# A later landing estimate for w2's size passes, attention work ahead of forced steps, and w2's sums ahead of the next group's

## The chip, the cores and the metric

The kernel runs on one core of one Trainium2 chip. The metric is the device time of one execution in microseconds; the kernel before took 1533.35 us (median of three runs). The engines are TensorE (PE, with its weight load PEld), VectorE (DVE), ScalarE (ACT), GpSimd (POOL) and SyncE (SP, which here issues nearly all loads). The TensorE clock was granted in full (1.00) throughout.

## The reference

Two layers act on x of 2048 tokens and 1024 features. Each adds first an attention branch (A) and then a gated feed-forward branch (B), both on a layer-normalised input. All weights are shared by the two layers.

```python
def A(x, wqkv, wo):                       # 32 heads of 32
    q, k, v = split(x @ wqkv)             # 1024 -> 3 x 1024
    # token s sees tokens s, s-2, ..., s-14 (8 of them, masked below 0)
    attn = softmax(sum_d(q[s] * k[s - off]) * 32 ** -0.5)
    return sum_w(attn * v[s - off]) @ wo  # 1024 -> 1024
def B(x, w1, w3, w2):                     # 1024 -> 3584 -> 1024
    return (silu(x @ w1) * (x @ w3)) @ w2

x = x + A(layernorm(x)); x = x + B(layernorm(x))    # layer 0
x = x + A(layernorm(x)); x = x + B(layernorm(x))    # layer 1
```

## The kernel before

**Stages.** The tokens are cut into four chunks of 512. First comes layer 0's query, key and value projection for all chunks (`q_part`, products L836, copies out of PSUM L840), 0 to 192 us. Then follow eight units u = 0 to 7, one for each layer and chunk, which do branch B (`b_stage`). Attention for the next unit runs meanwhile on DVE (`score_steps`: products L590, maximum L625, difference L628, exponential on ACT L629, sum L634, reciprocal L636, quotient L637; `value_steps`: L665; folds L510, L512, L514), with the projection wo on PE as `o_tile` (L771, added to x in L776). From u = 1 on, layer 1's projections for one chunk come between two units.

**Two forms of branch B.** Units 0 and 1 (to 514 us) multiply with w1 (L1279), w3 (L1288) and w2 (L1310) as they are. During them the other engines prepare weights for units 2 to 7. These use a scheme of seven products on 2 x 2 blocks in place of eight (P1 to P7, run by `pipeline` L1052 and, for w2, by `W` L1165), which needs sums and differences of weight blocks, kept in DRAM. In the seven-product form ACT copies or applies silu to product sums between the products (L1064, L1069, L1073, L1227, L1232; for w2 L1173, L1181, L1185), DVE adds (L1076, L1088, L1236; L1188), and PE's next product waits for these where it reuses a PSUM bank. P7, for instance, adds to the bank that L1073 (or L1185 for w2) has copied out after P6.

**Preparing the weights.** For a group of w1 or w3, `weight_size` squares the tile on ACT (L878) to size a scale; PE sums over partitions into a side bank, DVE reduces it (L884). `weight_sums` scales four blocks on ACT (L910), `differences` forms three more on DVE (L923), and POOL stores them. For w2 the size comes from the whole matrix: `part_of_w2` loads eight pieces of w2 in layer 0's projection stage into the idle tile hT (L973), and `measure2` squares each piece in two passes on ACT (L958). After the sixteenth pass `total_scale` (L993) makes the scale. Only then can `sums_of_w2` (L1009 on ACT, L1015 on DVE) form w2's blocks, from w2 tiles that unit 0 or 1 has loaded (L722).

**Order.** PE, DVE, ACT and SP execute in the order in which the program emits instructions, which Python settles when the kernel is built. `now` is a clock of estimates with one time for each of `pe`, `dve`, `act`, `sp` and `dma`; the functions of those names advance it. Work that isn't in the main chain stands in queues of generators, which yield an estimated cost, a time when ready, and the step. `background(until)` takes the DVE queues' steps (`makes`, `norms`, `adds`, `values`, `scores`) that fit before a time. `act_background()` takes ACT steps from `acts`, `sizes` (L958), `parts` (L878) and `reads` (L910, L1009), each while its estimated end lies no more than 2.2 us past PE's clock:

```python
if s is None or max(now["act"], s[1]) + s[0] > now["pe"] + gate[0]:
    break
```

`head(queue)` gives a queue's first step, or nothing when that generator is blocked. `release_held` frees w1 and w3 tiles once their group's sums are all emitted; `held` lists the (matrix, group) pairs that wait for that, `made` those that are done, and `finish_sums(done)` forces steps from `reads`, `parts` and `makes` until it is so. PSUM has six banks for the main products and two side banks, for `po` (L771), for the attention logits and for the sizes. Loads into SBUF go through SP's one queue: weights (L707 wqkv, L712, L718, L722), the transposes of normalised tokens (xn from L269 on DVE, or L318 and L345 on ACT; L272 transposes on a DMA), and attention's reads.

Of the kernel before, what the change touches and what calls it, by code (L numbers as in the profile page):

```python
# [17 lines left out]
def kernel(  # L18
# [95 lines left out]
    def head(queue):  # L114

        while queue:
            item = queue[0]
            if item[1] is None:
                item[1] = next(item[0], StopIteration)
                if item[1] is StopIteration:  # L120
                    queue.pop(0)
                    continue
            if item[1] == "blocked":
                item[1] = None
                return None
            return item[1]
        return None
# [173 lines left out]
    adds, acts, makes, reads, parts, sizes = [], [], [], [], [], []  # L301
# [53 lines left out]
    def take_act(queue):  # L355
        cost, ready, emit = queue[0][1]
        act(cost, ready)
        queue[0][1] = None
        emit()
# [338 lines left out]
    def load_weight(pieces=1):  # L698

        if len(w_tiles) == len(seq):  # L700
            return
        kind, i, n, *rest = seq[len(w_tiles)]
        if kind == "qkv":
            w = wp.tile([P, KH, D], BF16, name="wqkv", tag="w")
            step = KH // pieces
            for k0 in range(0, KH, step):
                nc.sync.dma_start(w[:, k0:k0 + step, :],  # L707
                                  wqkv_v[:, n * KH + k0:n * KH + k0 + step, i * D:(i + 1) * D])
            at = dma(1024, now["pe"]) if len(w_tiles) > 5 else 33.0
        elif kind == "t2":  # L710
            w = wp.tile([P, 8, 512], FP16, name="t2", tag="w")
            nc.sync.dma_start(w[:, 0:rest[0], :], t2_d[i][:, n])  # L712
            at = dma(128 * rest[0], now["pe"])
        elif kind in ("early", "late"):
            early = kind == "early"
            w = wp.tile([P, 2, 4 if early else 3, KT // 2, P], FP16, name=kind, tag="w")
            v = t_d[i][n][:, 0:8] if early else t_d[i][n][:, 8:14]
            nc.sync.dma_start(w[:], v.rearrange("p (a b) k c -> p a b k c", a=2))  # L718
            at = dma(1024 if early else 768, now["pe"])
        elif kind == "w2":  # L720
            w = wp.tile([P, 8, 512], BF16, name="w2t", tag="w")
            nc.sync.dma_start(w[:, 0:n, :], w2_v[:, i:i + n, rest[0] * 512:(rest[0] + 1) * 512])  # L722
            at = dma(128 * n, now["pe"])
        else:
            w = wp.tile([P, KT, FG * P], BF16, name=kind + "t", tag="w")
            v = w1_v if kind == "w1" else w3_v
            nc.sync.dma_start(w[:, :, 0:n * P], v[:, :, i * P:(i + n) * P])
            at = dma(1200, now["pe"])
            if rest[0]:
                got = {}  # L730
                parts.append([weight_size(*rest[0], w, at, got), None])
                reads.append([weight_sums(*rest[0], w, got), None])
        w_at[len(w_tiles)] = at
        w_tiles.append(w)

# [194 lines left out]
    def finish_sums(done):  # L930

        while not done():
            if head(reads) is not None:
                take_act(reads)
            elif head(parts) is not None:
                take_act(parts)
            elif head(makes) is not None:
                take(makes)
            else:
                pe_requests(1, True)  # L940

# [23 lines left out]
    def part_of_w2():  # L965

        i = len(w2_parts) - len(unread)
        while len(measured) < 2 * i:
            assert head(sizes) is not None
            take_act(sizes)  # L970
        if unread:
            g0, n, hh = unread.pop(0)
            nc.sync.dma_start(hT[:, 0:n, :], w2_v[:, g0:g0 + n, hh * 512:(hh + 1) * 512])  # L973
            sizes.append([measure2(i, n, dma(128 * n, now["pe"])), None])

    unread = list(w2_parts)

# [275 lines left out]
    def b_stage(u, hold):  # L1253

        l, c = units[u]
        last = l == 1
        ready = ready_norm(("B", l, c))
        xnT = xnTs[("B", l, c)]
        for (f0, f1) in fsplits:
            lastsplit = (f1 == fsplits[-1][1])  # L1260
            if u >= TU:
                products(u, f0, f1, hold)
                continue
            for g0 in range(f0, f1, FG):
                gn = min(FG, f1 - g0)
                w1t, w3t = weight("w1"), weight("w3")
                release_held(1)
                for fi in range(gn):
                    f = g0 + fi
                    slack = 1.0 if f < f1 - 2 else -0.5  # L1270
                    if f < f1 - 1:
                        between(hold)
                    else:
                        flush()
                    if f == 8 and 1 <= u and u + 3 < len(units):
                        queue_q(u + 3)
                    pg = bank("pg")
                    for kk in range(KT):
                        nc.tensor.matmul(pg[:], lhsT=w1t[:, kk, fi * P:(fi + 1) * P], rhs=xnT[:, kk, :],  # L1279
                                         start=(kk == 0), stop=(kk == KT - 1))  # L1280
                    r = pe(KT, ready)
                    sg = sgp.tile([P, CH], BF16, name="sg")
                    nc.scalar.activation(sg[:], pg[:], ACTF.Silu)
                    ts = act(0.5, r, "silu")
                    act_background()
                    pu = bank("pu")
                    for kk in range(KT):
                        nc.tensor.matmul(pu[:], lhsT=w3t[:, kk, fi * P:(fi + 1) * P], rhs=xnT[:, kk, :],  # L1288
                                         start=(kk == 0), stop=(kk == KT - 1))
                    r = max(pe(KT), ts)  # L1290
                    background(r + slack)
                    nc.vector.tensor_tensor(hT[:, f - f0, :], sg[:], pu[:], op=ALU.mult)
                    th = dve(0.64, r)
                    release_held(2)
                held.append((u, g0 // FG))
                release_held(1)
            if lastsplit:
                xnT_free["B", l, c] = now["pe"]
            split, nq = fsplits.index((f0, f1)), (f1 - f0) // 2
            flush()  # L1300
            got = [(weight("w2", False), w_at[used[0] - 1]) for _ in range(4)]
            release_held(1)
            tiles, times = [[[got[2 * hh + fh][i] for fh in range(2)] for hh in range(2)] for i in range(2)]
            for hh in range(2):
                now["pe"] = max(now["pe"], *times[hh])
                for j in range(TPC):
                    n, step = c * TPC + j, TPC * hh + j
                    acc = psum.tile([P, 512], FP32, name="acc", tag="mm")
                    for f in range(f1 - f0):
                        nc.tensor.matmul(acc[:], lhsT=hT[:, f, j * P:(j + 1) * P],  # L1310
                                         rhs=tiles[hh][f // nq][:, f % nq, :],
                                         start=(f == 0), stop=(f == f1 - f0 - 1))
                    pe(f1 - f0 - 1)
                    r = pe(1, th)
                    if step == 2:
                        release_held(0)
                    if step == 0:
                        steps = range(u * nq // 2, (u + 1) * nq // 2)
                        reads.extend([sums_of_w2(split, f, tiles, max(times[0] + times[1])), None] for f in steps)
                    act_background()  # L1320
                    background(r + 1.0)
                    dve(0.64, r)
                    xs = x_sb[:, n, hh * 512:(hh + 1) * 512]
                    nc.vector.tensor_tensor(xs, xs, acc[:], op=ALU.add)
                    if j == TPC - 1 and hh == 1:
                        finish_sums(lambda: all(("w2", split, f) in made for f in steps))
                        release(4)
                    between(hold and not lastsplit, lastsplit and hh == 0 and j == 1 and not hold)
        if u == TU - 1:
            force(makes, lambda: not any(pending))  # L1330
            scale_h()
            sums_free[:] = [0.0] * 3
# [80 lines left out]
```

## Time and profile before

| | us |
|---|---|
| median of three runs | 1533.35 |
| lowest, highest | 1532.43, 1533.71 |
| the profiled execution, its own time | 1532.7 |
| its span in the trace | 1531.0 |
| PE busy | 1518.1 (99%) |
| DVE busy | 1201.8 (78%) |
| ACT busy | 884.1 (58%) |
| POOL busy | 153.7 (10%) |

The span runs from the first to the last instruction in the trace; 1.7 us of the execution lie around it. A row of the timeline has the start and the duration in us, the engine, the line, the operation, and output and inputs by their names in the program; brackets give the idle time ahead of it and what ended it. A row of the waits has the waiting engine and line, what it waited for, total us, times and the longest. A row of the stretches has the length, the busy time of PE, PEld, DVE, ACT and POOL with counts, the granted clock, the DMA share and GB/s.

### The profile page before, as it was taken

What the parts mean: (1) busy time and instruction counts of PE and PEld (TensorE: products, weight loads), DVE (VectorE), ACT (ScalarE), POOL (GpSimd) and SP (SyncE); (2) the same over time, 40 slices, a digit from 0 to 9 for tenths busy, and PEclk for the clock granted to TensorE, in tenths of its full rate; (3) what the DMA queues carried; (4) which work ended last, traced back from release to release, by engine and by line L of the source; (5) the groups of instructions that cost most, each with busy time, mean ns of one, the idle gap of its engine ahead of it and who ended that gap; (6) DMA issues with size and microseconds to landing.
All of it is one profiled execution on the core that took longest, in us unless ns stands there. A gap on an engine that the chain in (4) does not pass through costs nothing.

```text
span 1531.0 us, 25095 instructions
## 1 busy us (share of the span) xinstructions
PE 1518.1 (99%) x9594; PEld 989.5 (65%) x9634; DVE 1201.8 (78%) x2126; ACT 884.1 (58%) x1388; POOL 153.7 (10%) x308
## 2 busy tenths in 40 slices
PE   9999999999999999999999999999999999999999
PEld 7666644444444577575786767766677767686865
DVE  4688998889989898989698958898678986435445
ACT  3885476567665357455565564756557445554643
POOL 1210102121211101001011010100111000000000
PEclk9999999999999999999999999999999999999999
DMA  9777969798997888979779997898969988878885
GB/s 321 202 218 215 253 226 330 272 304 289 306 320 247 280 316 294 347 264 303 263 269 324 346 268 282 280 323 302 323 225 333 338 296 282 306 272 334 318 294 203
DMA packets 261432, 439.56 MB, mean 287 GB/s; under 512 B 73856, under 2 KB 201088, under 8 KB 245056
## 3 DMA queue, kind: packets, MB, share of 16 engines
q1 hardware_dynamic: 248464, 390.90, 76.8%
q0 software_dynamic: 12704, 46.93, 8.6%
q8 instruction: 75, 1.23, 0.3%
q14 instruction: 45, 0.37, 0.1%
q10 hardware_dynamic: 144, 0.13, 0.0%
HBM read 345.90 MB, written 67.90 MB: 270 GB/s over the span
## 4 chain that ended last, share of the span: by engine, by line
PE 97%; ACT 1%; issue 1%; DVE 0%; DMA 0%; SPq 0%; ACTq 0%
PE st L1052 32%; PE ps L836 21%; PE w L1165 16%; PE po L771 7%; PE pg L1279 6%; PE pu L1288 6%; PE acc L1310 6%; PE pq L444 1%; PE L L604 0%; DMA wqkv<-in_A_wqkv_dram 0%; ACT L629 0%; ACT L1227 0%; ACT E L629 0%; ACT sg L1227 0%; DVE x_sb L1150 0%
## 5 line engine op out<-in xcount | busy, mean ns | idle before, releaser
L836 PE MATMUL ps<-xnT,wqkv 128*128 128x512 f16 (+1 forms) x1469 | 320.4, 379 | 0.2
L1052 PEld LDWEIGHTS <-early 128*128 128x128 f16 x2688 | 262.6, 98 | 40.4 <-issue 3.5
L836 PEld LDWEIGHTS <-wqkv 128*128 128x128 bf16 x1472 | 210.6, 144 | 108.1 <-issue 2.2
L1165 PE MATMUL w<-t,hT 128*128 128x512 f16 x1008 | 226.0, 379 | 0.6 <-ACT big L1185 0.5
L1052 PEld LDWEIGHTS <-late 128*128 128x128 f16 x2016 | 197.2, 98 | 30.6 <-issue 2.5
L590 DVE TENSOR_TENSOR tree<-qT,kT 128x2048 bf16<-128x2048 bf16 x128 | 156.3, 1221 | 35.8 <-DMA kT<-qkv_d 18.2
L1052 PE MATMUL st<-xnT,late 128*128 128x256 f16 x1344 | 174.2, 273 | 2.2 <-ACT big L1073 2.2
L510 DVE TENSOR_TENSOR tree<-tree 128x1024 bf16<-128x1024 bf16 x256 | 175.6, 686 | 0.9
L1052 PE MATMUL st<-big,early 128*128 128x256 f16 x1344 | 172.3, 273 | 1.6 <-ACT sg L1227 1.1
L1165 PEld LDWEIGHTS <-hT 128*128 128x128 f16 x1008 | 98.2, 98 | 112.9 <-DVE hT L1136 2.0
L1052 PE MATMUL st<-xnT,early 128*128 128x256 f16 x1344 | 165.7, 273 | 0.0
L665 DVE TENSOR_TENSOR tree<-At,vT 128x2048 bf16<-128x2048 bf16 x128 | 156.2, 1221 | 11.9 <-DMA At<-E 10.7
L1064 ACT COPY st<-st 128x512 f32<-128x512 f32 x84 | 48.3, 575 | 128.1 <-PE st L1052 127.4
L771 PE MATMUL po<-wo,oT 128*128 128x512 bf16 x486 | 110.8, 379 | 1.3
L840 ACT CAST hT<-ps 128x512 bf16<-128x512 f32 x96 | 55.8, 585 | 90.6 <-PE ps L836 88.3
L1288 PE MATMUL pu<-xnT,w3t 128*128 128x512 f16 x448 | 105.8, 379 | 0.0
L1279 PE MATMUL pg<-xnT,w1t 128*128 128x512 f16 x448 | 105.8, 379 | 0.0
L1310 PE MATMUL acc<-w2t,hT 128*128 128x512 bf16 x437 | 97.8, 379 | 0.6
L1076 DVE TENSOR_TENSOR st<-st,big 128x512 f32<-128x512 f32 x84 | 58.4, 695 | 46.9 <-ACT big L1073 46.8
L1227 ACT ACTIVATE sg<-st,down_scale 128x512 bf16<-128x512 f32 x126 | 86.6, 687 | 11.6 <-PE st L1052 11.0
L1052 PE MATMUL st<-big,late 128*128 128x256 f16 x672 | 87.1, 273 | 0.0
L771 PEld LDWEIGHTS <-oT 128*128 128x128 bf16 x512 | 50.1, 98 | 55.7
(167 smaller groups left out, 1916.6 us busy)
## 6 DMA issues: line engine op xcount, KB each, us to landing
early<-t_d SPq DMA_DIRECT2D x84, 1024.0 KB, 6.9
late<-t_d SPq DMA_DIRECT2D x84, 768.0 KB, 6.2
t<-t_d SPq DMA_DIRECT2D x42, 1024.0 KB, 7.3
t<-t_d SPq DMA_DIRECT2D x42, 768.0 KB, 5.3
wqkv<-in_A_wqkv_dram SPq DMA_DIRECT2D x28, 1024.0 KB, 8.1
w1t<-in_B_w_dram SPq DMA_DIRECT2D x14, 1024.0 KB, 7.6
w3t<-in_B_w_dram SPq DMA_DIRECT2D x14, 1024.0 KB, 11.0
t_d<-big POOLq DMA_DIRECT2D x28, 512.0 KB, 6.2
```

The lines of the kernel that those rows point to most:

```text
L510: nc.vector.tensor_tensor(b, b, buf[:, 4:8, :], op=ALU.add)
L590: V.tensor_tensor(pr, qT[:], kT[:, :, k0:k0 + TCH], op=ALU.mult)
L665: V.tensor_tensor(tm.rearrange("p w (a e) -> p w a e", a=4), At[:].rearrange("p a w e -> p w a e"), win, op=ALU.mult)
L771: nc.tensor.matmul(ps[:], lhsT=oT[:, t, j * P:(j + 1) * P], rhs=wo[:, t, hh * 512:(hh + 1) * 512], start=(t == 0), stop=(t == KT - 1))
L836: nc.tensor.matmul(ps[:], lhsT=ws[kk // KH][:, kk % KH, t::KT], rhs=xnT[:, kk, :], start=(kk == 0), stop=(kk == KT - 1))
L1052: nc.tensor.matmul(out[:, a, :], lhsT=w[:, a, blk, k, :], rhs=rhs[:, k, :], start=start and a == 0 and k == 0, stop=k == KQ - 1, skip_grou ...
L1076: nc.vector.tensor_tensor(G["D"][:], G["D"][:], su, op=ALU.add)
L1165: nc.tensor.matmul(out[:], lhsT=lhs[:, k, j * P:(j + 1) * P], rhs=w[:, k, :], start=start and k == 0, stop=k == nq - 1, skip_group_check=True)
L1227: nc.scalar.activation(sg[:], src, ACTF.Silu, scale=inv)
L1279: nc.tensor.matmul(pg[:], lhsT=w1t[:, kk, fi * P:(fi + 1) * P], rhs=xnT[:, kk, :], start=(kk == 0), stop=(kk == KT - 1))
L1288: nc.tensor.matmul(pu[:], lhsT=w3t[:, kk, fi * P:(fi + 1) * P], rhs=xnT[:, kk, :], start=(kk == 0), stop=(kk == KT - 1))
L1310: nc.tensor.matmul(acc[:], lhsT=hT[:, f, j * P:(j + 1) * P], rhs=tiles[hh][f // nq][:, f % nq, :], start=(f == 0), stop=(f == f1 - f0 - 1))
```

## The change

Three edits, all in the code that settles the order; no instruction of any engine is added or removed.

1. `part_of_w2` counts 3.0 us more until a piece of w2 has landed, so the size passes (L958) are seen as ready later.
2. `finish_sums` calls `background` up to the ready time of the step that it is about to force, ahead of that step. DVE steps from all five queues may thus be emitted there.
3. An item of `reads` carries its (matrix, group) key, and `sums_of_w2` items go in ahead of the first item whose group isn't in `held`, instead of at the end of the queue.

```diff
                 parts.append([weight_size(*rest[0], w, at, got), None])
-                reads.append([weight_sums(*rest[0], w, got), None])
+                reads.append([weight_sums(*rest[0], w, got), None, rest[0]])
...
         while not done():
-            if head(reads) is not None:
-                take_act(reads)
-            elif head(parts) is not None:
-                take_act(parts)
+            step = head(reads) or head(parts)
+            if step is not None:
+                background(step[1])
+                take_act(reads if head(reads) is not None else parts)
             elif head(makes) is not None:
-                take(makes)
+                background(head(makes)[1])
+                if head(makes) is not None:
+                    take(makes)
             else:
                 pe_requests(1, True)
...
             nc.sync.dma_start(hT[:, 0:n, :], w2_v[:, g0:g0 + n, hh * 512:(hh + 1) * 512])
-            sizes.append([measure2(i, n, dma(128 * n, now["pe"])), None])
+            sizes.append([measure2(i, n, dma(128 * n, now["pe"]) + 3.0), None])
...
                     if step == 0:
                         steps = range(u * nq // 2, (u + 1) * nq // 2)
-                        reads.extend([sums_of_w2(split, f, tiles, max(times[0] + times[1])), None] for f in steps)
+                        i = next((i for i, item in enumerate(reads) if item[2] not in held), len(reads))
+                        reads[i:i] = [[sums_of_w2(split, f, tiles, max(times[0] + times[1])), None, None] for f in steps]
```

## The prediction

> **What bounds the kernel now.** I read the page first, then TensorE's (PE's) waits, then its rows in stretches of 25 us, and last the timeline at each gap.
>
> ```profile
> span 1531.0 us, 25095 instructions
> PE 1518.1 (99%) x9594; PEld 989.5 (65%) x9634; DVE 1201.8 (78%) x2126; ACT 884.1 (58%) x1388; POOL 153.7 (10%) x308
> ...
> PE 97%; ACT 1%; issue 1%; DVE 0%; DMA 0%; SPq 0%; ACTq 0%
> ```
>
> PE is busy for 1518.1 of 1531.0 us and is 97% of the chain that ended last. So only idle time of PE can be won, and only new idle time of PE can be lost: the change removes no matmul. Where that idle time lies:
>
> ```profile
> PE st L1052 <- ACT big L1073: 2.2, 1, 2.2
> PE pq L444 <- DMA wqkv<-in_A_wqkv_dram: 1.4, 2, 0.7
> PE pw L200 <- DVE tree L195: 1.2, 1, 1.2
> PE st L1052 <- ACT sg L1227: 1.1, 1, 1.1
> ```
>
> Columns: total us, times, longest. The two middle rows belong to the first 10 us, ahead of everything the change touches. In the stretches, PE is 25.00 or 24.9 of 25 almost everywhere; two stretches stand out:
>
> ```profile
> 650.00:675.00 25.00, 23.86 (x202) 19.39 (x202) 18.65 (x34) 15.38 (x23) 2.27 (x4) 1.00 0.78 255
> 975.00:1000.00 25.00, 22.81 (x176) 16.56 (x174) 19.96 (x35) 19.90 (x32) 5.08 (x11) 1.00 1.07 329
> ```
>
> With the timeline I find six stalls of PE after the start: 1.25 us at 667.8, 0.19 at 878.1, 2.36 at 987.3, 0.63 at 1065.2, 0.28 at 1159.5, 0.57 at 1233.4. Sum 5.3 us, which is the most that any reordering can win. The wait that the change is named for is elsewhere, on ScalarE (ACT):
>
> ```profile
> ACT hsum L958 <- DMA hT<-in_B_w_dram: 13.3, 4, 3.7
> ```
>
> These 13.3 us lie between 126 and 192 us, where PE runs the layer 0 projections without a gap.
>
> **What the skill says.** The Trainium skill, "Perfetto Trace Analysis", section Identifying the Most-Contended Engine, warns that matmul busy share is no good measure of distance to the limit, because pipelined TensorE instructions look smaller in a trace than they are; its section Optimization Strategy says to look at the gaps between slices instead. This trace agrees: the page's 12.9 us of not-busy PE hold only about 8.2 us of real stalls (5.3 and the start's 2.9), the rest being slivers and missing records. So I count gaps. "ScalarE: Activation LUTs", section What ACT_TABLE_LOAD costs, gives 1283 ns for a load and 1380 ns for a drain with it. The trace has the 1283 ns (1.28 below) but no drain: the load at 665.19 begins 0.01 us after the copy before it ends. I use 1.28. "DMA: Bandwidth & Descriptors", section Issuing engines are not separate DMA queues, says that all issuers share the same 16 DMA engines, so a late-issued load lands later if others are moving. The trace agrees: the 1 MB wqkv loads of L707 land 5.7 to 15.0 us after issue, median 8.1.
>
> **Part 1: three more microseconds.** No instruction is added. In the two programs' orders the sixteen L958 passes (27.2 us in all) stand one to five L840 evacuation copies later on ACT (0.585 us each, so 0.6 to 2.9 us of copies pass ahead). The copies no longer queue behind a pass that waits for its DMA, so much of the 13.3 us of ACT waiting goes. PE: 0 us, since the projection products of L836 cover it: they show no wait for the copies there. A late pass delays the next piece's load into hT by up to 2.9 us and the scale of w2 (L993) alike; L993 runs at 195.9 us and the first L1009 that uses its scale at 264.6, 69 us later. Without that cover the cost would be at most those 2.9 us.
>
> **Part 2: attention work ahead of forced steps.** finish_sums now first emits whatever DVE steps fit. Every DVE and ACT step behind moves: exponentials (L629, each 1.28 + 0.60 + 1.28 us with its two table loads) change place between the evacuations that PE waits for. **Part 3** moves w2's combinations (L1009, L1015) ahead of the next group's L910. Durations of the moved steps are the page's; the sum of the two parts, place by place, follows.
>
> A, 667.8 us. The profile before:
>
> ```profile
> 665.19 1.28 ACT L629 ACT_TABLE_LOAD   x1
> 666.49 0.60 ACT L629 ACTIVATE E<-L 128x512 bf16<-128x512 f32 x1
> 667.10 1.28 ACT L1227 ACT_TABLE_LOAD   x1
> ...
> 668.39 0.69 ACT L1227 ACTIVATE sg<-st,down_scale 128x512 bf16<-128x512 f32 x1
> ...
> 669.13 1.03 PE L1052 MATMUL st<-big,early 128*128 128x256 f16 x8 [1.09 <-ACT sg L1227]
> ```
>
> PE waits for the L1227 that queues behind the exponential. Afterwards L1227, L1232 and L1064 stand ahead of the exponential: **-1.25**. Late next is L1069 behind it, which has a product's length of room.
>
> B, 987.3 us. The exponential moves five ACT steps earlier and the L345 pass (1.24) nine later, so the 2.2 us wait for L1073 goes. But the exponential's 3.16 us now falls where L1073, L1232, L1227 and L1064 have slack of 0.4 to 1.0 each; carrying the delay along gives waits of 0.75, 0.65, 0.1 and 0.9. **0** (from -1.9 to +0.5).
>
> C, 588 to 604 us. The exponential comes two places earlier, without the output projection's matmuls (3.4 us) that covered it: **+0.2** (0 to 1).
>
> D, 815 to 822 us. The exponential comes six ACT places earlier, and on DVE L634, L636, L637 and L590 (1.03 + 0.55 + 0.69 + 1.22 = 3.5) then stand ahead of L1188. The next L1185 needs the buffer that L1188 reads, and P7 of the down product needs that copy (819.82 before, needed by 821.5): **+0.6** (0 to 2).
>
> E, 802 us. Before and after differ by one exchange:
>
> ```profile
> 801.63 0.58 ACT L1073 COPY big<-st 128x512 f32<-128x512 f32 x1
> 802.10 1.25 ACT L345 ACTIVATE xn<-x_sb,mom 128x1024 f16<-128x1024 bf16 x1
> 803.24 0.69 ACT L1227 ACTIVATE sg<-st,down_scale 128x512 bf16<-128x512 f32 x1
> ```
>
> L345 now goes first: L1073, whose result PE takes at 802.72, ends one step (1.14) later, at 803.4: **+0.7**.
>
> F, 215, 387 and 394 us. The reduction L884 frees the side bank that the projection output (po) takes next. It is emitted 0.43 later at 215, where it had 0.12 of room (+0.3); at the other two places four L241 steps, 2.6 us, partly precede it (+0.35 together): **+0.65** (0 to 1.5).
>
> G, 514 us. On SP's queue two transposes (L272) now stand ahead of the two wqkv loads (L707). Before:
>
> ```profile
> 486.77 4.14 SPq L707 DMA_DIRECT2D wqkv<-in_A_wqkv_dram  x2
> 506.05 12.03 SPq L272 DMA_TRANSPOSE xnT<-xn  x4
> ```
>
> The loads were issued at 486.8 and 490.5 and first used at 514.2 and 515.1. Now they wait behind transposes that wait for DVE's xn (L269). Adding the DVE steps ahead of xn, it is ready near 501.8 instead of 505.5; the transposes' issue takes 1.27 + 2.95, so the loads go out at about 506.3 and 506.9. With 5.7 us to landing they are in time, with the median 8.1 they land at 514.4 and 515.0, with 10 they are 2 us late: **+0.5** (0 to 3). Behind them on SP are only the next transposes; PE's L836 waits for the loads and everything waits for PE. Two w2 loads (L722) also fall behind transposes near 301 and 380, with 15 us to spare: 0.
>
> POOL's stores follow L923 and L1015 and keep over 10 us of lead: 0. The stalls at 1065, 1159 and 1233 keep their order on every engine: 0.
>
> **Sum.** -1.25 + 0 + 0.2 + 0.6 + 0.7 + 0.65 + 0.5 = +1.4 us. The profiled execution took 1532.7 us (span 1531.0 and 1.7 around it), so it becomes 1534.1; the median of the runs, 1533.35, lies 0.65 above the profiled one, so the median becomes **1534.7**. 0.2% is 3.1 us, about what a measurement of this kernel can tell from no change.
>
> **Rivals.**
> 1. *Hidden altogether.* The clock's estimates only reshuffle cover; A's gain and the small losses cancel. For it: PE is 25.00 in most stretches. Against it: E is an exchange with no cover. 1533.3.
> 2. *Faster.* A and B go (-1.25 - 2.36) and no new place stalls: 1533.35 - 3.6 = 1529.7. For it: the exponential leaves both longest waits. Against it: 3.16 us on ACT must go somewhere, and at B the places it goes to have under 1.0 of slack.
> 3. *Slower: the queue blocked on SP at 514 us.* If xn becomes ready after 503 or the loads need over 8 us, PE stands still for what is over. At 10 to 14 us to landing (the row's range reaches 15.0) this is 2 to 6 us on top of the other +0.9: 1536.2 to 1540.2, say 1538. DVE speaks for it: it is busy 21 to 25 of each 25 us there, and the pulled-ahead attention steps (1.2 us each) push xn back by about one step apiece. Against it: the before's loads just behind, at 518.2 and 518.8, landed in 5.7 and 7.8.
> 4. *The change doesn't do what it says.* The later estimate cannot let a pass start earlier than its data; if only part 1 mattered, nothing would move: rival 1's time.
>
> **How the numbers follow.** Forecast 0.45 (1532.5 to 1537, nearly all within 0.2%: 0.40 same, 0.05 slower); hidden 0.10 (same); faster 0.10 (0.09 faster, 0.01 same); slower by SP or by several of C to F at their upper ends 0.35 (slower). Together faster 0.09, same 0.51, slower 0.40. The range leaves out half of the faster case and the tail beyond 1540: 1530.3 to 1540.2.
>
> **What would show it.** Right: the wait for L1227 near 667 gone; at 802 a wait of PE for L1073 of 0.7; at 815 to 822 one for L1185; wqkv issued after 506 and PE's wait for it at 514 under 1 us; ACT's wait in L958 well under 13.3 with PE unmoved at 192 us. Wrong: a wait for wqkv of over 2 us (rival 3), a longest PE wait at 980 to 990 below 0.5 with none new at 802 or 818 (rival 2), or any new stall before 200 us, which would mean that part 1 is not free.

## The result and the profile after

The changed kernel takes **1548.42 us** (median of four runs, 1547.67 to 1549.94) against 1532.89 for the kernel before on the same chip: a ratio of **1.0103**, 95% interval 1.0086 to 1.0121. It is 15.5 us slower; the forecast was 1534.7, with 1540.2 as its upper end. The profiled execution took 1548.78.

From line 940 on, line numbers are two higher than in the kernel before (L958 is now L960, L1052 is L1054, L1288 is L1290, L1310 is L1312). The page, its head and its chain:

```profile
span 1547.0 us, 25133 instructions
PE 1526.7 (99%) x9634; PEld 989.7 (64%) x9634; DVE 1201.4 (78%) x2126; ACT 883.4 (57%) x1388; POOL 160.5 (10%) x308
...
PE 59%; DVE 5%; ACT 3%; DMA 3%; issue 1%; POOL 0%; SPq 0%; ACTq 0%; DVEq 0%; POOLq 0%
```

The span is 16.0 us longer, and PE's share of the chain fell from 97% to 59%: other engines, DMAs and issue now stand in it with 12% together, and the view leaves the rest open. PE busy also rose by 8.6 us, though PE has the same work in both programs: 5.0 us of it are matmuls at half speed, shown below, and the trace of before lacks 40 records (9594 of 9634), each of which reads as some 0.05 us of idle time (0.432 us between the starts around it, 0.379 us busy). So I count waits and slow matmuls again, not busy time. The waits after (total us, times, longest):

```profile
ACT hsum L878 <- DMA w3t<-in_B_w_dram: 7.8, 1, 7.8
...
ACT hsum L960 <- DMA hT<-in_B_w_dram: 5.6, 3, 2.9
PE ps L836 <- DMA wqkv<-in_A_wqkv_dram: 5.4, 2, 3.2
```

and the stretches that stand out, with the work of the two that stood out before, which comes 17 us later here:

```profile
450.00:475.00 25.00, 20.05 (x79) 8.18 (x78) 18.15 (x39) 16.57 (x26) 2.88 (x4) 0.86 0.89 304
525.00:550.00 25.00, 21.04 (x92) 12.29 (x93) 10.82 (x21) 7.42 (x12) 0.00 (x0) 0.86 1.08 345
667.00:692.00 25.00, 25.00 (x216) 20.50 (x214) 19.35 (x38) 15.91 (x25) 2.14 (x4) 1.00 0.81 279
992.00:1017.00 25.00, 23.78 (x176) 16.98 (x174) 20.63 (x34) 18.34 (x28) 4.38 (x11) 1.00 1.01 321
```

The stall at 667 is gone, and the one at 987 is small. Two new stretches are bad, and in both the granted clock (the column after POOL) is 0.86, not 1.00. The timeline of PE in the first:

```profile
466.62 3.59 PE L1290 MATMUL pu<-xnT,w3t 128*128 128x512 f16 x8 [4.52 <-DMA w3t<-in_B_w_dram]
470.01 3.19 PE L1281 MATMUL pg<-xnT,w1t 128*128 128x512 f16 x8
473.03 1.89 PE L1290 MATMUL pu<-xnT,w3t 128*128 128x512 f16 x8
```

PE waits 4.52 us for a w3 tile. After that wait, sixteen matmuls take 473.03 - 466.62 = 6.41 us where two products of eight otherwise take 3.45 (2 x 8 x 0.216): fourteen of them start 0.427 us apart. **The wait costs 4.5 us and its slow matmuls 3.0 more.** The second stretch, first SP's queue and then PE:

```profile
511.30 4.29 SPq L272 DMA_TRANSPOSE xnT<-xn  x2
515.64 1.95 SPq L707 DMA_DIRECT2D wqkv<-in_A_wqkv_dram  x2
```

```profile
525.79 1.08 PE L836 MATMUL ps<-xnT,wqkv 128*128 128x512 f16 x4 [2.25 <-DMA wqkv<-in_A_wqkv_dram]
530.04 15.11 PE L836 MATMUL ps<-xnT,wqkv 128*128 128x512 f16 x60 [3.17 <-DMA wqkv<-in_A_wqkv_dram]
```

The first wqkv pair goes out 29 us later than before (515.6 against 486.8), behind the transposes, and PE waits 5.4 us for them; nine slow matmuls add 2.0.

**Where the 16.0 us lie**, by the ends of matching stages in the two traces: -0.65 up to 353 us (nearly all of it a later start in the one profile of before); +7.1 and -6.9 around 400 us, where 6.9 us of PE work changed sides and nothing is lost; **+9.6** from 444 to 496 us; **+7.8** in the projection that follows (514 to 573); -0.9 in all the rest.

### The profile page after: what moved, and what is told of

Read it like the earlier page. It is cut to its first block, busy times and chain, and to the rows that moved or that the text cites. A ratio compares the mean times of both kernels' runs of the same rounds, so it can differ in the third digit from the quotient of the medians.

```text
span 1547.0 us, 25133 instructions
## 1 busy us (share of the span) xinstructions
PE 1526.7 (99%) x9634; PEld 989.7 (64%) x9634; DVE 1201.4 (78%) x2126; ACT 883.4 (57%) x1388; POOL 160.5 (10%) x308
## 4 chain that ended last, share of the span: by engine, by line
PE 59%; DVE 5%; ACT 3%; DMA 3%; issue 1%; POOL 0%; SPq 0%; ACTq 0%; DVEq 0%; POOLq 0%
PE st L1054 28%; PE w L1167 14%; PE ps L836 11%; PE po L771 4%; DMA t_d<-big 1%; DMA w3t<-in_B_w_dram 1%; DMA wqkv<-in_A_wqkv_dram 1%; PE pu L1290 1%; ACT sg L1229 1%; DVE tree L510 0%; DVE tree L665 0%; DVE hT L1238 0%; DVE tree L590 0%; ACT big L910 0%; DVE hT L1138 0%
## 5 line engine op out<-in xcount | busy, mean ns | idle before, releaser
L1054 PEld LDWEIGHTS <-early 128*128 128x128 f16 x2688 | 262.6, 98 | 39.2 <-issue 2.2
L1054 PEld LDWEIGHTS <-late 128*128 128x128 f16 x2016 | 197.1, 98 | 30.4 <-issue 2.4
L1054 PE MATMUL st<-xnT,late 128*128 128x256 f16 x1344 | 174.2, 273 | 1.1 <-ACT big L1075 1.1
L1054 PE MATMUL st<-big,early 128*128 128x256 f16 x1344 | 172.2, 273 | 0.8 <-ACT st L1066 0.7
L1054 PE MATMUL st<-xnT,early 128*128 128x256 f16 x1344 | 166.0, 273 | 0.0
L1066 ACT COPY st<-st 128x512 f32<-128x512 f32 x84 | 48.3, 575 | 128.2 <-PE st L1054 127.5
L771 PE MATMUL po<-wo,oT 128*128 128x512 bf16 x512 | 116.0, 379 | 0.1
L1290 PE MATMUL pu<-xnT,w3t 128*128 128x512 f16 x448 | 107.5, 383 | 4.9 <-DMA w3t<-in_B_w_dram 4.5
L1312 PE MATMUL acc<-w2t,hT 128*128 128x512 bf16 x448 | 97.8, 379 | 0.0
L1229 ACT ACTIVATE sg<-st,down_scale 128x512 bf16<-128x512 f32 x126 | 86.5, 687 | 11.9 <-PE st L1054 11.7
L1054 PE MATMUL st<-big,late 128*128 128x256 f16 x672 | 87.1, 273 | 0.0
L771 PEld LDWEIGHTS <-oT 128*128 128x128 bf16 x512 | 50.1, 98 | 55.7 <-issue 0.7
```

The lines of the kernel that those rows point to most:

```text
L771: nc.tensor.matmul(ps[:], lhsT=oT[:, t, j * P:(j + 1) * P], rhs=wo[:, t, hh * 512:(hh + 1) * 512], start=(t == 0), stop=(t == KT - 1))
L1054: nc.tensor.matmul(out[:, a, :], lhsT=w[:, a, blk, k, :], rhs=rhs[:, k, :], start=start and a == 0 and k == 0, stop=k == KQ - 1, skip_grou ...
L1229: nc.scalar.activation(sg[:], src, ACTF.Silu, scale=inv)
L1312: nc.tensor.matmul(acc[:], lhsT=hT[:, f, j * P:(j + 1) * P], rhs=tiles[hh][f // nq][:, f % nq, :], start=(f == 0), stop=(f == f1 - f0 - 1))
```

## The experiments

The quoted expectations were written before their runs. In them S is the theory that the order of SP's queue makes the loss (loads behind transposes), O that it is the place of two projection tiles, and R that it is the place of one size pass; what these are is shown as it comes up. The kernel before was timed again beside each of the four groups of runs (medians 1533.03, 1533.45, 1533.48 and 1533.09 us), and each ratio is against those runs.

**p1: edit 1 alone.** Only `dma(128 * n, now["pe"]) + 3.0`.

> Edit 1 alone: the 3.0 us more on the landing estimate, with finish_sums and reads as before. Theory S (SP's queue: the longer estimate pushes the clock of loads on, and with it the order in which transposes, attention reads and weight loads stand on SP, up to 520 us): this program has the same SP order around the two stalls as the full change, so it carries the loss, about 1549 us (before + 15 to 17), with PE's waits for w3t near 465 and for wqkv near 525. Rival F (the attention work that finish_sums pulls ahead is to blame): 1533, within 2 us of before, no such waits.

Measured: 1553.44 us, ratio 1.0132 (1.0117 to 1.0147). PE waits 5.1 us for w3t and 5.6 for wqkv at the same two places, and the stalls at 667 and 987 us stay. Edit 1 alone carries the whole loss.

**p2: edit 2 alone.** Only the hunk in `finish_sums`.

> Edit 2 alone: finish_sums calls background first, estimate and reads as before. Theory S: SP's order around 380 to 520 us is that of before, so no late load; it keeps only what the change won and lost elsewhere, about 1532 (before - 1, the 1.25 us stall at 667 gone). Rival F: 1545 or more, with the waits for w3t and wqkv. The forecast's places C to F, if real, would show here too, as +1 to +3.

Measured: 1532.03 us, ratio 0.9997 (0.9988 to 1.0005): no change. No late loads; the waits of 2.2 us for L1075 and 1.1 for L1229 are those of before. In the two traces every engine has the same instructions in the same order: edit 2 alone yields the kernel before, and this run times it once more. So edit 2 by itself moves none of what the prediction gave it. Edit 3 was not run by itself: the order of every engine is the same with and without it, alone as well as in the full change.

**x1 and x2: SP's order put back at one place each**, in the full change. A transpose (L272), as a function `turn`, is held in a list and issued behind the loads that it had overtaken (the lines that do the latter are left out here).

```diff
-                nc.sync.dma_start_transpose(out=xnT[:, :, j * P:(j + 1) * P], in_=xn)
+            if key == ("B", 0, 2) and r == 0:   # x1: behind the wqkv pair; x2: ("Q", 1, 0), behind w2 loads
+                late_turns.append(turn)
+            else:
+                turn()
...
```

> The full change, but the two transposes of unit 2's tokens (L272) are issued on SP only after the first two wqkv loads of layer 1, as before; every other engine's order is unchanged. Theory S: the loads go out near 500 instead of 515.6, PE's waits for wqkv at 525 (2.25 + 3.17 us) and the half-speed matmuls after them (2.0 us) go: about 1541 (after - 7 to - 8). Rival D (the loads land late because the DMA engines are busy, not because they are issued late): less than 2 us gained, 1546 to 1548.

Measured: 1543.75 us (1539.46 to 1549.12), ratio 1.0070 (1.0048 to 1.0093). The two waits for wqkv are gone altogether, and 4.7 us of the median with them (the ratio's interval still overlaps the changed kernel's a little). The profiled execution was the slowest and had others in their place: 2.0 us for L884's result at 388, 2.2 at 455, 5.0 for w3t.

> The full change, but the transposes of the next projection's tokens (L272, near 397 us) are issued on SP behind the w2 loads (L722) that they now stand ahead of; every other engine's order is unchanged. Theory S: the w2 loads go out near 380 to 390 instead of 402, the pile of transfers at 402 to 432 spreads out, w3t lands before 440, ACT's 7.8 us wait in L878 shrinks below 2, and PE's waits near 449 and 466 (1.0 + 4.5 us) with the half-speed stretch (3.0 us) go: about 1539 (after - 8.5 to - 9.5). Rival A (ACT's order, the size pass L878 standing ahead of eight sums L1009, is to blame whatever SP does): the stall near 466 stays, 1547 to 1549.

Measured: 1545.22 us, ratio 1.0079 (1.0064 to 1.0094); more was expected. The wait for w3t shrank from 4.5 to 2.9 us, but the w1 and w3 loads went out as late as in the changed kernel.

**x3: SP's order put back at all three places**, the attention reads of qT and kT behind the twelfth w3 load too.

> The full change with SP's order put back by hand at three places: w2 loads (L722) ahead of the transposes near 397 us; the w1 and w3 loads (L727) of unit 1's second half ahead of attention's qT and kT reads (L547), which wait for DVE; and the first two wqkv loads ahead of unit 2's transposes. PE, DVE, ACT and POOL keep the full change's order. Theory S (SP's order is the whole cause): w3t lands before 435, no wait of PE for w3t or wqkv is left, about 1532 (1530 to 1534). Rival A (the DVE and ACT orders that edit 1 leaves also cost, by a late po near 388 or by L878 ahead of L1009): 1536 to 1542.

Measured: 1543.25 us, ratio 1.0064 (1.0049 to 1.0079). No wait for wqkv is left, but the wait for w3t stays at 4.8 us. What the w1 and w3 loads (L739 here) waited for is in the waits of SP's queue:

```profile
SPq L739 <- ACT big L1031: 20.7, 2, 19.9
SPq L739 <- ACT big L930: 13.5, 1, 13.5
```

L930 is the scaling on ACT (L910 elsewhere) that must have read a tile before it is loaded again, L1031 the same for w2 (L1009 before). The first w3 load that is late waits 13.5 us for ACT. The load that PE waits for comes behind the wait of 19.9 us and goes out at 453.0 us, as late as in the changed kernel (453.1). With SP's order mended the loads wait for ACT instead. So **S holds for the second stretch and falls for the first**.

**fill: work that nobody needs in front of the late product.** Added to the full change: twenty matmuls on wo into pu, ahead of the product that waits.

```diff
+                    if (u, f) == (1, 20):
+                        for _ in range(20):
+                            nc.tensor.matmul(pu[:], lhsT=wo[:, 0, 0:P], rhs=wo[:, 0, 0:512], start=True, stop=True)
```

> The full change plus twenty 128x512 matmuls of no use (wo by wo into the bank that the next product clears) on PE just ahead of the product that waits for w3t near 466 us: 20 x 0.216 = 4.3 us of work laid into a wait of 4.5. Theory C (the half-speed matmuls after the stall come from PE's being idle, not from the late data): the wait shrinks to about 0.2 and the fourteen matmuls at 0.427 us behind it run at 0.216: about 3 us gained, 1545.4. Rival (the slow matmuls are due to something else, such as the transfers then under way): no gain, 1548 to 1549.

Timeline of PE at the place (L1291 is the added work, L1293 the w3 product):

```profile
464.95 4.48 PE L1291 MATMUL pu<-wo 128*128 128x512 bf16 x19
469.45 1.90 PE L1293 MATMUL pu<-xnT,w3t 128*128 128x512 f16 x8
471.18 1.89 PE L1281 MATMUL pg<-xnT,w1t 128*128 128x512 f16 x8
472.91 1.89 PE L1293 MATMUL pu<-xnT,w3t 128*128 128x512 f16 x8
```

The sixteen matmuls now take 472.91 - 469.45 = 3.46 us, so the slow ones come from PE's idleness and not from the data. But the total is 1549.91 us, ratio 1.0110 (1.0092 to 1.0127): no better. The profiled execution had lost 2.5 us more ahead of the place (1.3 us for w3t at 448, 2.2 for L878's result at 452, where the changed kernel has 1.0), and it waits 6.2 us for wqkv afterwards against 5.4. Why nothing of the 3 us shows in the median was not followed further.

**pad0_5 and pad6_0: 0.5 and 6.0 in place of 3.0 us.**

> The full change with 0.5 us more in place of 3.0. Its orders on PE, DVE, POOL and SP are those of the full change, ACT's differ only in layer 0's size passes. Theory S: the loss is that of one order of SP's queue, not of an amount of waiting: about 1548, as with 3.0. Rival P (the loss grows with the microseconds added): a sixth of it, about 1535.

> The full change with 6.0 us more in place of 3.0. The planner then comes to another order: on SP the w1 and w3 loads of unit 1's second half stand ahead of qT and kT, and the first two wqkv loads ahead of unit 2's transposes, as before. Theory S: no late w3t and no late wqkv, about 1532 to 1535. Rival P (the loss grows with the microseconds added): 1555 or more.

Measured: 1547.79 us, ratio 1.0097 (1.0080 to 1.0115), and 1554.04 us, ratio 1.0138 (1.0122 to 1.0153). Half a microsecond costs as much as three, and the two have the same order on PE, DVE, POOL and SP. With 6.0 the order is another: the tiles are late again (429.7 us) and the loads at 410 and 490 us are in order on SP, but new waits appear elsewhere (6.0 us for w3t at 251, 2.7 for L884's result at 305, 2.7 for w2t at 426), so S, which expected no loss here, missed by some 20 us. The microseconds don't scale the loss; they select the order that the planner falls into.

**Which order?** The full change and p2 differ in many places on ACT and DVE, from layer 0 on. Two differences ahead of the first late load move a whole link of the weight preparation or PE work of some length, and these were tested. Two projection tiles (`o_tile`, L771, rows of 16 matmuls and 3.6 us) stand behind products 37 and 38 instead of 44 (pairs of a w1 and a w3 product, counted through units 0 and 1; unit 1 begins with the 29th). And one size pass on ACT (L878, the 18th) stands behind eight sums (L910) instead of ahead of them. The tiles on PE, before and then after:

```profile
412.97 3.62 PE L771 MATMUL po<-wo,oT 128*128 128x512 bf16 x16
```

```profile
384.55 3.61 PE L771 MATMUL po<-wo,oT 128*128 128x512 bf16 x16
...
391.60 3.84 PE L771 MATMUL po<-wo,oT 128*128 128x512 bf16 x16
```

**y1: the full change with the size pass in its old place; y2: edit 2 alone with the size pass moved.** In `act_background`:

```diff
+            if queue is reads and 363.9 < now["pe"] < 367.4:   # y1 (y2: queue is parts, 367.4 to 370.9)
+                continue
```

> The full change, but act_background takes no sums (L910) while PE's estimated clock is between 363.9 and 367.4, so that the second size pass (L878) of the ninth weight group goes ahead of eight sums again, as before. Everything after that point is planned anew. Theory R (the preparation of weights is a ring without slack: size pass, scale, sums on ACT, differences on DVE, store, buffer free, next sums, tile free, next load; eight sums ahead of one size pass near 364 made it late by 4, 6, 9 and then 12 us, and PE pays when its tiles run out): the differences of block 24 come near 385 again instead of 396, w1 and w3 loads 23 and 24 near 410 to 415, and the loss of the first stretch goes: 1532 to 1538. Theory S (SP's order as such): w1 and w3 loads still stand behind qT and kT here, wqkv behind two transposes: 1540 to 1548.

> Edit 2 alone (measured at the time of before), with the one swap put in: no size pass is taken while PE's estimated clock is between 367.4 and 370.9, so that the second size pass of the ninth group goes behind eight sums, some 7 us later. No 3.0 us anywhere. Theory R: block 24's differences come 6 to 12 us later than the 383 of edit 2 alone, the ring stays late, PE waits for w3t near 466: 1541 to 1550. Rival (the loss needs more than this, such as the other order of layer 0 and unit 0 that edit 1 makes): 1531 to 1535.

y1: 1540.01 us, ratio 1.0045 (1.0028 to 1.0061). No wait for w3t; for wqkv 5.0 us in two waits, 3.9 the longer, and thirteen slow matmuls remain. The tiles are at 385.0 and 392.0 us still. y2: 1550.19 us (1543.62 to 1552.20), ratio 1.0104 (1.0080 to 1.0128), without any microsecond added: one size pass moved by hand brings a loss of the same size. But in y2 the planner, from the clocks that this leaves, also puts the two tiles early (behind products 41 and 42), so y2 doesn't tell the two apart.

**z: lateness without a change of order.** Edit 2 alone, and fourteen copies on POOL ahead of one store of a block in `differences`.

```diff
+        if len(blocks_done) == 17:
+            for k in range(14):
+                nc.gpsimd.tensor_copy(b[:, k % 7], b[:, k % 7])
```

> Edit 2 alone, with fourteen copies of no effect on POOL (each block of big onto itself, 128x512) ahead of one single store of w-differences near 384 us: the orders of PE, DVE, ACT and SP and the planner's clock are those of edit 2 alone. It delays one store by perhaps 7 to 14 us. Theory R: a delay at one point of the ring goes round: the sums that wait for that buffer, and every later store, come about as late, and PE loses what the tiles in hand do not cover, 3 to 10 us: 1535 to 1542. Theory S, or a ring with slack: the delay is absorbed, 1532 to 1533.5.

The timeline of POOL:

```profile
382.31 9.26 POOL L930 COPY big<-big 128x512 f16<-128x512 f16 x14 [4.42 <-DVE big L924]
391.52 0.55 POOL L931 DMA_DIRECT2D t_d<-big  x1
```

The store goes out at 391.5 us, 7.8 later than in p2 (383.7). The next three blocks are 2.7, 3.8 and 3.8 us late, the two after them 1.9, later ones 1.4, and unit 1's w1 products are not late at all. 1534.06 us, ratio 1.0004 (0.9996 to 1.0013): absorbed.

**y4: the full change, but no projection tile while the planner's PE clock is between 380 and 409 us.**

```diff
-        while o_queue and (must or oT_at.get((o_queue[0][0], o_queue[0][1] // 2), 1e9) + 0.3 <= now["pe"]):
+        while o_queue and (must or not 380.0 < now["pe"] < 409.0 and oT_at.get(...) + 0.3 <= now["pe"]):
```

> The full change, 3.0 us and all, but the two projection tiles (L771, 6.9 us of PE together) that it puts behind products 37 and 38 of unit 1's first half may not be emitted while PE's estimated clock is between 380 and 409; the planner then puts them behind product 44, among w2's products, as before and as edit 2 alone does. Theory O (the early tiles push the weight preparation 6.9 us back against PE, and their norms, transposes and reads take the places ahead of weight loads on SP): no wait for w3t near 466 and none for wqkv near 525, 1531 to 1534. Rival R (the eight sums ahead of one size pass near 364, which stay in this program, carry the first stretch): a wait for w3t of 2 us or more stays, 1537 to 1545.

Measured: **1533.70 us, ratio 1.0006 (0.9998 to 1.0015)**: the whole loss is gone. In PE's timeline the size matmuls (L892), which follow the size passes, stand where the changed kernel has them (380.82, 384.41 there), and the tiles where the kernel before has them:

```profile
380.67 0.28 PE L892 MATMUL size<-size,ones 128*128 128x2 f32 x2
384.26 0.28 PE L892 MATMUL size<-size,ones 128*128 128x2 f32 x2
...
412.16 3.62 PE L771 MATMUL po<-wo,oT 128*128 128x512 bf16 x16
```

Its longest waits are those of before:

```profile
PE st L1054 <- ACT big L1075: 2.2, 1, 2.2
...
PE st L1054 <- ACT sg L1229: 1.1, 1, 1.1
```

The four kernels make a table (ratio to before):

| | size pass in its old place | size pass behind eight sums |
|---|---|---|
| tiles behind product 44 | p2 (the kernel before): 0.9997 | y4: 1.0006 |
| tiles behind products 37 and 38 | y1: 1.0045 | changed kernel: 1.0103 |

Without the early tiles there is no loss with either place of the size pass; with them there is, and the size pass decides whether the first stretch joins in. **O stands for this order and R alone falls.** (Each cell is planned anew from the moved step on. So y4 shows that the place of the two tiles decides, but not how much of the loss is their own and how much that of the orders that follow from it: in y4 the first two wqkv loads also stand ahead of the transposes again, at 484.2 and 492.6 us. What pad6_0 loses, with late tiles, is another matter, and its cause was not followed further.)

**y1x1: both repairs, y1's and x1's, with the tiles early.**

> The full change with both of the earlier single repairs: the size pass near 364 ahead of the sums again (which alone removed the wait for w3t), and the first two wqkv loads ahead of unit 2's transposes on SP (which alone removed the wait for wqkv). If the two stretches are all of the loss: 1531 to 1533.5, before less about 1. If something given back later remains (weights still 4 to 14 us late after the first repair): 1535 to 1540.

Measured: 1536.76 us, ratio 1.0032 (1.0019 to 1.0045). No wait for w3t; small ones are left (1.4 us for L884's result, 1.3 for wqkv, 2.1 for a DVE sum at 569). Mending the two places that show the waits leaves 3.7 of the 15.5 us; not putting the tiles early leaves none that can be told from noise. No kernel beat the one before by more than its interval.

## Why the prediction was wrong, and where it was right

**The chain.** Adding 0.5 or 3.0 us in layer 0 tips the planner's clocks so that two projection tiles of the next unit go out seven and six products early in unit 1, 28 us earlier in the trace (384.55 against 412.97). That they are what decides, y4 shows. How they do it I read from the traces. The weight preparation stands among unit 1's products in every engine's order: size pass, reduction, sums, differences, store, release of the tile, next load. ACT's sums (L910) stand behind the silu (L1285) of a product that now comes after a tile, so ACT stands still for the tile as well. ACT's timeline in the changed kernel, then the same steps in y4:

```profile
389.93 0.60 ACT L1285 ACTIVATE sg<-pg 128x512 bf16<-128x512 f32 x1 [3.34 <-PE pg L1281]
390.42 3.16 ACT L910 ACTIVATE big<-w3t,up_scale 128x512 f16<-128x512 bf16 x5
397.20 0.60 ACT L1285 ACTIVATE sg<-pg 128x512 bf16<-128x512 f32 x1 [3.62 <-PE pg L1281]
397.70 0.71 ACT L910 ACTIVATE big<-w3t,up_scale 128x512 f16<-128x512 bf16 x1
```

```profile
386.34 0.58 ACT L1285 ACTIVATE sg<-pg 128x512 bf16<-128x512 f32 x1
386.82 3.16 ACT L910 ACTIVATE big<-w3t,up_scale 128x512 f16<-128x512 bf16 x5
...
390.36 0.71 ACT L910 ACTIVATE big<-w3t,up_scale 128x512 f16<-128x512 bf16 x1
```

The moved size pass makes the first two links late (18th pass +3.6 us, 370.3 against 366.6; a reduction L884 +5.9). In y4 these are late too (+4.6 and +6.6), and it comes to little: sums +5.0, differences +5.2, the w3 load +4.8 and the w1 load not late. With the tiles the lateness grows instead: sums of the next blocks +8.6, differences +11.7, and the w1 and w3 loads +15.2 and +14.5. The loads, before and then after, from SP's timeline:

```profile
409.68 4.05 SPq L727 DMA_DIRECT2D w1t<-in_B_w_dram  x1
413.83 3.29 SPq L727 DMA_DIRECT2D w3t<-in_B_w_dram  x1
```

```profile
424.87 3.32 SPq L727 DMA_DIRECT2D w1t<-in_B_w_dram  x1
428.29 3.65 SPq L727 DMA_DIRECT2D w3t<-in_B_w_dram  x1
```

ACT waits 7.8 us for the second of these tiles in L878, with eight sums (L1011) queued behind it. The next four loads are 10 to 16 us late as well and go out within 2.9 us of one another (451.9 to 454.8). The second of them is the w3 tile that PE waits for; it lands after 13.5 us, at 466.6. Its issue before, in y1 and after:

```profile
439.09 0.37 SPq L727 DMA_DIRECT2D w3t<-in_B_w_dram  x1
```

```profile
447.30 0.37 SPq L729 DMA_DIRECT2D w3t<-in_B_w_dram  x1
```

```profile
453.12 0.37 SPq L727 DMA_DIRECT2D w3t<-in_B_w_dram  x1
```

The first pair of loads alone doesn't decide: in y1 it is 14.3 and 11.4 us late too, yet the load at 447.3 is early enough and PE waits for no w3t. Nor does ACT's wait of 7.8 us: in x3 it shrinks to 0.4, and PE's wait stays. How the first stretch's loss divides among the moved steps on ACT, DVE and PE stays open: x3 excludes SP's order, y1 and y4 each remove it. The second stretch is a loss of its own: in y1, without the first, PE still waits 5.0 us for wqkv.

By the prediction's own steps:

- **"Part 1 … PE: 0 us" is the step that failed.** At its place it was right: PE shows no wait before 192 us, and ACT's wait in the size passes fell from 13.3 to 5.6 us. But I took an estimate on the planner's clock to act only where its instruction stands. The same clock decides everything emitted later, and p1 shows the whole loss from this one number. The sign that I had set for this, a new stall before 200 us, didn't come: the loss lies at 444 us and later.
- **Part 2 got moves that it doesn't make by itself.** p2 leaves A and B as they were. The two stalls also stay in p1 (early tiles without edit 2) and in y4 and pad6_0 (edit 2 with late tiles); they are gone or small in every run that has edit 2 and early tiles. Part 3 moves nothing.
- **"Two w2 loads (L722) also fall behind transposes near 301 and 380, with 15 us to spare: 0" is in doubt too**: x2 puts such loads back in front of their transposes and is 3.2 us faster than the changed kernel by the medians, but the two ratios' intervals just overlap. The step priced a shift in SP's order against the old times, and the prediction names nowhere the two tiles that moved in PE's order beside it. Its sum had no term for 444 to 496 us, where 9.6 us lie.
- **A right**: -1.25 forecast; the exponential now stands behind L1234 and L1066 (L1066 at 684.55, its table load at 685.14), and the stretch 667 to 692 is 25.00. **B**: 0 forecast; the stall of 2.36 became one of 0.53 us at the same product (1005.87) with two of 0.38 and 0.27 ahead of it, and the stage ends give about -0.5. **C, D**: no wait at either place, against +0.2 and +0.6. **E**: the exchange is there (L345 at 817.20, then L1075), but PE waits for L1075 0.17 us at 818.97 and not 0.7.
- **F**: no wait in this profile, +0.65 forecast; x1 and x2 show one of 2.0 us for L884's result at 388 us, beyond the bound of 1.5.
- **G: right place and order, the landing too short.** +0.5 forecast with an upper end of 3, +7.8 measured. The loads went out at 515.6, 9.3 us after the forecast 506.3, but PE came to their product as much later (523.5 against 514.2), so they had the 7.9 us that the forecast gave them. It took the median of 8.1 us for the landing; the two loads took 10.1 and 12.9 (from the view of wqkv, 505 to 530 us):

```profile
DMA to landing us min/median/max: 10.1/11.5/12.9
```

In y1 the loads go out at 506.5, as forecast, and land after 9.1 and 12.7 us, and PE waits 5.0. Rival 3 had priced 10 to 14 us of landing at 2 to 6, and the wait is 5.4. The 2.0 us of slow matmuls after it stood in no sum. x1 shows the block's weight: 4.7 us of the median.

- **The reading of the 12.9 us in which PE isn't busy** put what isn't a stall down to slivers and missing records. In fact 1.2 us lie ahead of the first matmul and 3.5 behind the last; the slivers are some 2.2. The forecast doesn't hang on it.

## What to carry to other kernels

Where a program's order comes from a planner that keeps one clock, price a changed estimate by the orders it yields on every engine, not by the place where it is added: look for whole tiles of the main engine that moved, then follow from them which buffers come free later. See first whether an edit changes any order at all: edit 2 alone and edit 3 anywhere changed none here. Lateness in time was absorbed (7.8 us at a store cost nothing), while 6.9 us of PE work put earlier in the order, with the orders that followed from it, cost 15 us: an engine that waits for PE in its own order holds up all that stands behind. Mending the visible waits one at a time moves them on; find the first thing that is late.

## What the hardware showed beyond that

**An idle PE can restart at half speed.** After the 4.5 us wait, fourteen matmuls of 128x512 started 0.427 us apart, then 0.216 again: 3.0 us on top of the wait. The Trainium skill, "TensorE: Matmul & The Clock Gate", Part 1, has these two figures (426.7 and 215.7 ns) and says that the clock halves after an idle window of about 3.4 us, in windows that run free. The figures agree, and so do the windows: wherever the half clock occurs within the fifteen traces, it holds for 3.4 or 6.8 us, and it need not begin when PE resumes. In the changed kernel it began 0.8 us ahead of that (466.62), in y4 0.9 us after it (990.65); the granted clock is the third number from the end:

```profile
465.79:472.62 6.83, 6.00 (x15) 2.14 (x16) 5.41 (x11) 6.83 (x11) 1.10 (x2) 0.50 1.09 356
```

```profile
991.55:994.97 3.42, 3.42 (x11) 1.18 (x9) 3.38 (x7) 1.34 (x2) 0.33 (x1) 0.50 0.95 386
```

The length of the gap does not quite agree: slow matmuls followed waits of 2.9 us (x2 at 464) and 2.0 us (x1 at 388) too. One wait of 2.19 us, the old one at B, stands in several traces with the same product behind it. PE's timeline in the kernel before, then in y4:

```profile
990.66 1.89 PE L1165 MATMUL w<-t,hT 128*128 128x512 f16 x8
```

```profile
991.52 3.58 PE L1167 MATMUL w<-t,hT 128*128 128x512 f16 x8
```

The same eight matmuls took 1.7 us more in one execution (8 x 0.211) and nothing more in the other; this wait was followed by the half clock in y4 and p1, and not in the kernel before, p2, z and pad6_0. Over all traces, single waits of up to 1.9 us brought no slow matmuls, those from 2.0 to 2.9 us some and some not, and every one of 3.6 us or more did, for 1.5 to 3.0 us on top of itself. A longer wait isn't dearer: p1's of 5.1 us cost 1.5 on top, the changed kernel's of 4.5 us 3.0.

**A 1 MB load takes longer in a bunch.** Four loads of w1 and w3 that went out over 9.0 us in the kernel before (436.0 to 444.9) landed after 6.8, 11.1, 11.7 and 12.8 us; the same four went out within 2.9 us in the changed kernel (451.9 to 454.8) and landed after 5.5, 13.5, 15.8 and 17.7. The pair of wqkv loads took 8.9 to 13.2 us in the four traces in which it went out within 1.5 us behind the transposes (changed kernel, p1, y1, y2), against the median of 8.1 on the page of before. No run here holds all other transfers equal, but a forecast that uses a median of the page for a bunched stretch is too short.
